# Crossbar transfers for the attention output of four batches, copies moved to ScalarE, and a new order, in a linear-attention and gated-convolution kernel

## The chip, the cores and the metric

The kernel runs on one core of one Trainium2 chip. A core has TensorE (PE, matrix products), VectorE (DVE), ScalarE (ACT), GpSimd (POOL) and SyncE (SP), which work side by side and wait for each other by semaphores; sixteen DMA engines move data for all of them. The metric is the device time of one execution in microseconds (us); lower is better. Several executions are timed, and one more view of one of them, a profile, lists every instruction with its start and duration.

## The reference

Two layers follow each other, over 8 batches of 576 positions. The first is attention by random features with 8 heads of 64 dimensions and 128 features; the second multiplies two projections with a third one that was convolved along the sequence.

```python
def phi(x):                       # q and k are scaled by D ** -0.25 before
    proj = einsum('bhsd,md->bhsm', x, omega)
    h = proj - sum(x * x, -1, keepdims=True) / 2
    return exp(h - max(h, -1, keepdims=True)) / sqrt(m)

q_p, k_p = phi(q_s), phi(k_s)
kv = einsum('bhsm,bhsd->bhmd', k_p, v)
z = sum(k_p, axis=2)
attn = einsum('bhsm,bhmd->bhsd', q_p, kv) / (einsum('bhsm,bhm->bhs', q_p, z)[..., None] + 1e-6)

x = attn.transpose(0, 2, 1, 3).reshape(B, S, H * D)
x1, x2, x3 = split(x @ w_proj, 3, axis=-1)
x2_conv = irfft(rfft(x2, axis=1) * rfft(filter_fft, axis=0)[None], n=S, axis=1)
out = (x1 * x2_conv * x3) @ w_out
```

All inputs and the output are float32; the kernel computes in bfloat16 with float32 sums.

## The kernel before

**The order of the work.** The kernel is written as two plain functions, `attention()` (line 931) and `hyena()` (line 1199). Neither sends an instruction to the chip. A recording layer, `Plan`, takes every call, with the stage and batch that the last `nc.at(stage, b)` named. `Plan.order` then gives each instruction a due time from its dependencies and from hand-set numbers by stage (`LEAD`), by stage and batch (`SHIFT`) and by stage and engine (`LEAN`), with `PERIOD`, `STRETCH` and `STAY` for the whole. `Plan.simulate` steps through a model of the engines and picks what goes next on each; `issue()` at line 383 sends the calls in that order. Each engine executes its own list in order, so an instruction that waits holds up all behind it on its engine. Because all calls are sent from one line, the profile has nearly all instructions at L388; they are told apart by the names of their tiles.

**Attention.** Of each batch 512 positions are the main part, four tiles of 128; the last 64 positions of two batches go together as one "left" tile. POOL loads `kn`, `qn`, `vn` (and `kl`, `ql`, `vl`) and casts them to bfloat16 on the way. Keys and queries must have their head dimension on the partitions, in `kt` and `qt`, for the feature products with `om2`. In batches 0 to 3 TensorE transposes them (`turn_keys`, `turn_queries`, through a PSUM bank named `t` and a copy). In batches 4 to 7 (`crossed`, line 310) a crossbar transfer, a DMA that transposes, does it from SP: `cross`, lines 951, 1020 and 1025. ScalarE takes the exponentials (`ek`, `eqt`). `max_to_c` finds the largest feature of each key, in the work tile `h1` with one buffer, and `scale_values` divides the values by it (`vc`). Key sums `kv` of 8 heads by 64 dimensions and one normaliser each, 520 columns, are copied out of PSUM at line 1119. `vcl`, `ekl` and `eql` are the same for the left tiles.

**Turning the output** (stage "turn out", lines 1146 to 1175). For each of the four tiles of a batch, eight matmuls make numerators and normaliser of eight heads in two PSUM banks (`two_banks`, tiles named `a`), and `normalise` (line 892) divides: a reciprocal and one multiplication on VectorE, into a tile `xb` of 128 positions by 512 channels. The second layer needs channels on the partitions, in `xt`. For batches 0 and 1 `turn_runs` does it by matmuls with a rearranged target; for batches 2 to 7 `turn_back` (line 908) makes eight transposes into one bank `t` for two tiles, and ScalarE copies 1,024 columns into `xt`.

**The second layer** goes by pairs of batches. `fold` and `fold_rest` add and subtract thirds of the sequence (`xf`, `xfl`), `project2` multiplies with the middle third of `wproj`, `forward` transforms by matmuls with tables, `spectrum` multiplies by the filter, the stage "inverse" transforms back, `gates` (line 1239) makes the product of the first and third projection (`x13`) from `xt` directly, and the stage "out" multiplies with `wout` and stores from `osb` tiles (three buffers), by SP. The filter is transformed once at the start (`filter_transform`); `split_out` (line 799) copies three of its results out of PSUM, a 128-row part on ScalarE and the negated lower half on VectorE, before SP moves them into `hps` and `hqs`.

**PSUM.** Matmul results stand in three single banks `h`, two pairs `a` and one bank `t`. A bank is free for the next product when ScalarE or VectorE has read it.

Of the kernel before, what the change touches and what calls it, by code (L numbers as in the profile page):

```python
# [11 lines left out]
FP32 = mybir.dt.float32  # L12
BF16 = mybir.dt.bfloat16
# [3 lines left out]
ALU = mybir.AluOpType  # L17
# [2 lines left out]

P = 128

PERIOD, STRETCH, STAY = 110.779, 7.132, 996.75
LEAD = {
    "cross keys": -8.69, "cross queries": -12.1, "filter": 3.6, "fold": 1.32, "forward": 26.46,
    "gates": -2.05, "inverse": 2.98, "keys": -44.78, "left keys": -2.87, "left out": -0.28,
    "left queries": 0.38, "load filter": -15.08, "load k": 17.16, "load kl": -0.85,
    "load q": 9.83, "load ql": -0.81, "load v": 8.12, "load vl": 0.04, "load w0": -1.42,
    "load w1": -2.9, "load w2": 1.71, "out": -19.09, "queries": -0.66, "residues": -3.04,
    "rest": -35.96, "start": -94.12, "sums": 14.75, "tables": -1.88, "turn out": 0.42,  # L30
    "turn queries": 4.98, "values": 204.41, "zeros": 3.6,
}

SHIFT = {
    ("forward", 0): -17.5, ("forward", 2): -35.59, ("forward", 7): 31.65, ("gates", 1): -47.99,
    ("gates", 2): -78.23, ("keys", 6): 46.62, ("keys", 7): 50.83, ("left queries", 1): -15.18,
    ("load kl", 0): -29.99, ("load ql", 0): 28.1, ("load v", 0): -89.26, ("queries", 6): -56.89,
    ("rest", 1): 278.3, ("rest", 7): 50.04, ("sums", 2): -15.61, ("sums", 6): -36.73,
    ("sums", 7): -24.35, ("turn out", 2): -115.3, ("turn out", 6): 1.26, ("values", 0): -174.25,
    ("values", 2): -204.34,  # L40
}
LEAN = {
    ("fold", "DVE"): -17.73, ("forward", "DVE"): 11.02, ("forward", "PE"): 2.87,
    ("gates", "PE"): 97.94, ("inverse", "DVE"): 14.74, ("keys", "PE"): -60.85,
    ("queries", "PE"): -5.83, ("rest", "PE"): -2.62, ("sums", "PE"): -3.28,
    ("turn out", "DVE"): -5.95, ("turn out", "PE"): -24.15,
}

SIZE = {FP32: 4, INT32: 4, BF16: 2, FP16: 2, mybir.dt.uint32: 4}
# [342 lines left out]
def kernel(  # L392
# [11 lines left out]
    nc = Plan(tc.nc, tc)  # L404
    B, H, S, D = q.shape
# [4 lines left out]
    NS = 2  # L410
    NT = 4
# [4 lines left out]
    CB = DM // P  # L416
# [3 lines left out]
    GAIN = 64.0  # L420
# [4 lines left out]
    att = ctx.enter_context(tc.tile_pool(name="att", bufs=1))  # L425
# [3 lines left out]
    def two_banks():  # L429
        return nc.tile(psum, [P, 2, 512], FP32, name="a2", bufs=2)  # L430
# [90 lines left out]
    for j in range(2):  # L521
        nc.vector.tensor_scalar_mul(
            out=om2[j * D : (j + 1) * D, :], in0=omt[:D, :MF], scalar1=qk_scale
# [32 lines left out]
    lo64, hi64 = slice(0, 64), slice(64, 128)  # L556

    residues = {}
# [240 lines left out]
    def split_out(ps, c):  # L799


        sc_ = nc.tile(hy, [P, 2, DM], BF16, name="osb", bufs=3)
        nc.scalar.mul(out=sc_[:, 0], in_=ps[:], mul=fsc[:, 0:1] if c == 1 else 2.0 * GAIN / S)
        nc.vector.tensor_scalar(
            out=sc_[hi64, 1], in0=ps[hi64, :], scalar1=-2.0 * GAIN / S, scalar2=None, op0=ALU.mult
        )
        moves = (
            (hps, slice(0, 64), 0, slice(0, 64)),
            (hps, slice(64, 128), 0, slice(0, 64)),
            (hqs, slice(0, 64), 1, slice(64, 128)),  # L810
            (hqs, slice(64, 128), 0, slice(64, 128)),
        )
        if c == 1:
            moves = (
                (hps, slice(0, 64), 0, slice(0, 64)),
                (hps, slice(64, 65), 0, slice(64, 65)),
                (hps, slice(65, 128), 0, slice(1, 64)),
                (hqs, slice(1, 64), 1, slice(65, 128)),
                (hqs, slice(65, 128), 0, slice(65, 128)),
            )  # L820
        for dst, rows, x, of in moves:
            nc.sync.dma_start(out=dst[rows, c, :], in_=sc_[of, x, :])
# [66 lines left out]
                out=ek_out, in_=ps[:].rearrange("p j (g m) -> p j g m", m=MF), func=AF.Exp  # L889
            )  # L890

    def normalise(ps):

        psh = ps[:, :, 0 : 4 * (D + 1)].rearrange("p a (h c) -> p a h c", c=D + 1)
        rden = nc.tile(att, [P, 2, 4, 1], FP32, name="rden", bufs=3)
        nc.vector.reciprocal(out=rden[:], in_=psh[:, :, :, D : D + 1])
        xb = nc.tile(att, [P, CB, P], BF16, name="xb", bufs=4)
        nc.vector.tensor_tensor(
            out=xb[:].rearrange("p c (g d) -> p (c g) d", d=D).rearrange(
                "p (a h) d -> p a h d", a=2  # L900
            ),
            in0=psh[:, :, :, 0:D],
            in1=rden[:].to_broadcast([P, 2, 4, D]),
            op=ALU.mult,
        )
        return xb
# [10 lines left out]
    def turn_runs(xt, xbs, c):  # L917


        ps = bank_t()  # L920
        for t in range(NT):
            nc.tensor.matmul(
                out=ps[:].rearrange("p (x t) -> p t x", t=NT)[:, t],
                lhsT=xbs[t][:, c],
                rhs=ident[:],
                start=True,
                stop=True,
            )
        nc.scalar.copy(out=xt[:, c, 0:SM], in_=ps[:])

    def attention():
        ekl = None
        for i in range(B // 2):
# [5 lines left out]
            for bb in range(2):  # L939
                b = 2 * i + bb  # L940
# [8 lines left out]
                crossed = b >= B // 2  # L949

                def cross(dst, src):
                    nc.sync.dma_start_transpose(out=dst, in_=src)
# [121 lines left out]
                for two in ((0, 1), (2, 3)):  # L1074
                    made = []
                    for pr in two:
                        ps = two_banks()
                        made.append((pr, ps))
                        for j in range(2):
                            nc.tensor.matmul(  # L1080
                                out=ps[:, j, :],
# [6 lines left out]
                                start=True,  # L1088
                                stop=True,
                            )  # L1090
                    for pr, ps in made:
                        nc.scalar.activation(
                            out=eqt[:, pr].rearrange("p j t c -> p j (t c)")
                            if b >= NS
                            else eqt[:, pr].rearrange("p h (u j) c -> p j (h u) c", j=2),
                            in_=ps[:]
# [6 lines left out]
                ps = two_banks()  # L1103
                for h in range(H):
                    half = ps[:, h // 4]
                    o = half[:, (h % 4) * (D + 1) : (h % 4 + 1) * (D + 1)]
                    nc.tensor.matmul(
                        out=o, lhsT=ekl[:, h, :], rhs=vcl[:, bb, h, 0 : D + 1], start=True, stop=False
                    )
                    for t in range(NT):  # L1110
                        nc.tensor.matmul(
                            out=o,
                            lhsT=ek[:, h, t, :],
                            rhs=vc[:, h, t, 0 : D + 1],
                            start=False,
                            stop=(t == NT - 1),
                        )
                kv = nc.tile(att, [P, 2, 4, D + 1], BF16, name="kv", bufs=3)
                nc.vector.tensor_copy(
                    out=kv[:],  # L1120
                    in_=ps[:, :, 0 : 4 * (D + 1)].rearrange("p a (h c) -> p a h c", c=D + 1),
                )
# [2 lines left out]
                if bb == 1:  # L1125
# [3 lines left out]
                    ps = two_banks()  # L1129
                    for j in range(2):  # L1130
                        nc.tensor.matmul(
                            out=ps[:, j, :],
                            lhsT=om2[rows[j]],
                            rhs=qlt[rows[j]].rearrange("p g s -> p (g s)"),
                            start=True,
# [3 lines left out]
                    for j in range(2):  # L1139
                        hs = slice(j * SL, (j + 1) * SL)  # L1140
                        nc.scalar.activation(
                            out=eql[:, j, :, hs].rearrange("p (g a) s -> p a g s", a=2),
                            in_=psf[:, :, :, hs],
# [3 lines left out]
                xt = nc.tile(hy, [P, CB, SM], BF16, name="xt", bufs=4)  # L1147
                xt_tiles[b] = xt
                xbs = []
                for t in range(NT):  # L1150
                    ps = two_banks()
                    for h in range(H):
                        nc.tensor.matmul(
                            out=ps[:, h // 4, (h % 4) * (D + 1) : (h % 4 + 1) * (D + 1)],
                            lhsT=eqt[:, h // 2, h % 2, t, :],
                            rhs=kv[:, h // 4, h % 4, :],
                            start=True,
                            stop=True,
                        )
                    xb = normalise(ps)  # L1160
                    xbs.append(xb)
                    if b < NS:
                        if t == NT - 1:
                            for c in range(CB):
                                turn_runs(xt, xbs, c)
                    elif t % 2 == 1:
                        turn_back(
                            xt[:, :, (t - 1) * P : (t + 1) * P].rearrange(
                                "p c (g x) -> p g c x", g=2
                            ),  # L1170
                            xbs,
                            "p (g c) x -> p g c x",
                            g=2,
                        )
                        xbs = []
# [4 lines left out]
            xtl = nc.tile(hy, [P, 2, CB, SL], BF16, name="xtl", bufs=2)  # L1180
            ps = two_banks()
            for h in range(H):
                o = ps[:, h // 4, (h % 4) * (D + 1) : (h % 4 + 1) * (D + 1)]
                for j in range(2):
                    nc.tensor.matmul(
                        out=o,
                        lhsT=eql[:, j, h, :],
                        rhs=kv_tiles[2 * i + j][:, h // 4, h % 4, :],
                        start=(j == 0),
                        stop=(j == 1),  # L1190
                    )
            xb = normalise(ps)
# [347 lines left out]
```

## Time and profile before

| | |
|---|---|
| median of six executions | 269.28 us (267.62 to 270.65) |
| the profiled execution | 267.79 us, of which the span from its first to its last instruction is 265.8 us |
| granted TensorE clock in it | 0.992 |
| matmuls, weight loads | 2,266 each |
| transposes of `xb` on TensorE | 144 |
| copies of `xt` out of bank `t` on ScalarE | 12 of 1,024 columns, 8 of 512 |
| crossbar transfers | 8, on SP |
| moved by POOL's queue | 17.31 MB |
| moved by SP's and ScalarE's queue | 16.94 MB |

The profile is of one execution; the time beside its span is what lies around the first and last instruction. A line of a group reads: line, engine, operation, target and sources, tile shape and count, then busy time in us and the mean duration in ns, then idle time of the engine just before these instructions and what ended it. A slice is a fortieth of the span, and its digit the busy tenths. The end of a matmul is modelled, and matmuls overlap, so the busy time of TensorE is not the sum of its durations.

### The profile page before, as it was taken

What the parts mean: (1) busy time and instruction counts of PE and PEld (TensorE: products, weight loads), DVE (VectorE), ACT (ScalarE), POOL (GpSimd) and SP (SyncE); (2) the same over time, 40 slices, a digit from 0 to 9 for tenths busy, and PEclk for the clock granted to TensorE, in tenths of its full rate; (3) what the DMA queues carried; (4) which work ended last, traced back from release to release, by engine and by line L of the source; (5) the groups of instructions that cost most, each with busy time, mean ns of one, the idle gap of its engine ahead of it and who ended that gap; (6) DMA issues with size and microseconds to landing.
All of it is one profiled execution on the core that took longest, in us unless ns stands there. A gap on an engine that the chain in (4) does not pass through costs nothing.

```text
span 265.8 us, 5830 instructions
## 1 busy us (share of the span) xinstructions
PE 242.7 (91%) x2266; PEld 137.4 (52%) x2266; DVE 221.8 (83%) x492; ACT 194.8 (73%) x301; POOL 62.7 (24%) x86
## 2 busy tenths in 40 slices
PE   0267679999999999999999999999999999999994
PEld 0255536665556566454566455444855555455541
DVE  7889998769977889999989776999999886378780
ACT  1797487676999968799755896999646966756633
POOL 8823662372557303151014000000000000000000
PEclk9997999999999999999999999999999999999999
DMA  6999999999999997999979352515613123101406
GB/s 78 190 198 198 160 202 209 203 171 147 123 136 157 202 170 43 172 162 149 276 120 167 78 107 94 118 57 154 137 34 121 39 95 102 44 22 38 159 1 197
DMA packets 84707, 34.74 MB, mean 131 GB/s; under 512 B 56139, under 2 KB 79176, under 8 KB 84680
## 3 DMA queue, kind: packets, MB, share of 16 engines
q0 software_dynamic: 59616, 17.31, 64.1%
q1 hardware_dynamic: 24920, 16.94, 27.6%
q8 instruction: 17, 0.28, 0.4%
q10 hardware_dynamic: 144, 0.13, 0.1%
q14 instruction: 10, 0.08, 0.1%
HBM read 34.64 MB, written 9.44 MB: 166 GB/s over the span
## 4 chain that ended last, share of the span: by engine, by line
PE 76%; DVE 15%; ACT 6%; issue 2%; ACTq 0%; DVEq 0%
PE h L388 58%; PE a L388 12%; PE t L388 5%; DVE h L388 2%; ACT eqt L388 1%; DVE yt L388 1%; DVE vcl L388 1%; DVE bt L388 1%; ACT L388 1%; DVE xb L388 1%; ACT yt L388 1%; DVE xf L388 1%; DVE vc L388 1%; DVE x L388 1%; DVE qt L388 1%
## 5 line engine op out<-in xcount | busy, mean ns | idle before, releaser
L388 PE MATMUL h<-xt,wproj 128*128 128x512 bf16 x256 | 62.0, 380 | 0.0
L388 ACT CAST x<-h 128x512 bf16<-128x512 f32 x68 | 40.2, 599 | 27.0 <-PE h L388 25.4
L388 PEld LDWEIGHTS <-wproj 128*128 128x128 bf16 x384 | 31.2, 99 | 26.2 <-issue 1.3
L388 ACT ACTIVATE ek<-a 128x1024 bf16<-128x1024 f32 x32 | 32.0, 1042 | 3.6 <-PE a L388 3.6
L388 ACT ACTIVATE eqt<-a 128x1024 bf16<-128x1024 f32 x32 | 32.1, 1048 | 1.8 <-PE a L388 1.8
L388 PE MATMUL h<-wproj,xf 128*128 128x512 bf16 x128 | 31.2, 379 | 0.0
L388 PE MATMUL h<-wout,yt 128*128 128x512 bf16 x128 | 30.1, 379 | 0.3 <-DVE yt L388 0.3
L388 ACT ACTIVATE osb<-h 128x512 f32<-128x512 f32 (+3 forms) x46 | 25.9, 573 | 4.5 <-PE h L388 2.9
L388 POOL DMA_DIRECT2D qn<-in_q_dram x26 | 22.9, 895 | 26.0 <-DMA qt<-qn 14.0
L388 DVE TENSOR_TENSOR x<-h,x 128x512 bf16<-128x512 f32 x32 | 22.0, 688 | 6.9 <-PE h L388 6.5
L388 DVE TENSOR_TENSOR xb<-a,rden 128x512 bf16<-128x512 f32 x36 | 23.3, 675 | 0.3
L388 DVE TENSOR_TENSOR bt<-h,osb 128x384 f16<-128x384 f32 x32 | 16.6, 553 | 3.7 <-PE h L388 2.0
L388 PEld LDWEIGHTS <-yt 128*128 128x128 bf16 x128 | 12.0, 98 | 14.7 <-DVE yt L388 0.8
L388 PEld LDWEIGHTS <-xf 128*128 128x128 bf16 x134 | 12.4, 99 | 12.4 <-PE a L388 0.4
L388 PE MATMUL h<-x,fwb 128*128 128x512 bf16 x72 | 18.3, 379 | 0.0
L388 PE MATMUL h<-gtab,xs 128*128 128x384 bf16 x64 | 15.6, 326 | 0.3 <-DVE bt L388 0.3
L388 ACT COPY xt<-t 128x1024 bf16<-128x1024 bf16 x12 | 12.2, 1019 | 4.4 <-PE t L388 4.2
L388 PE MATMUL t<-ident,xb 128*128 128x128 bf16 x144 | 13.7, 238 | 0.8 <-ACT xt L388 0.8
L388 PEld LDWEIGHTS <-eqt 128*128 128x128 bf16 x256 | 10.8, 98 | 5.5 <-DVE xb L388 1.2
L388 PE MATMUL a<-om,kt 64*128 64x128 bf16 x256 | 11.8, 226 | 1.4 <-DVE kt L388 1.0
L388 PE MATMUL a<-kv,eqt 128*128 128x65 bf16 x256 | 11.9, 194 | 1.3 <-DVE xb L388 0.9
L388 DVE RECIPROCAL rden<-a 128x8 f32<-128x8 f32 x36 | 7.0, 201 | 7.2 <-PE a L388 6.6
(167 smaller groups left out, 472.1 us busy)
## 6 DMA issues: line engine op xcount, KB each, us to landing
out_dram<-osb SPq DMA_DIRECT2D x24, 256.0 KB, 2.1
vn<-in_v_dram POOLq DMA_DIRECT2D x8, 512.0 KB, 9.8
kn<-in_k_dram POOLq DMA_DIRECT2D x7, 512.0 KB, 7.3
qn<-in_q_dram POOLq DMA_DIRECT2D x24, 128.0 KB, 8.7
sw<-sp SPq DMA_DIRECT2D x16, 128.0 KB, 3.8
wproj<-in_moe_w_proj_dram POOLq DMA_DIRECT2D x3, 512.0 KB, 8.2
qn<-in_q_dram POOLq DMA_DIRECT2D x2, 512.0 KB, 12.6
out_dram<-xf SPq DMA_DIRECT2D x4, 256.0 KB, 2.0
```

Source lines behind the costliest of these rows:

```text
L388: getattr(real, name)(*args, **kw)
```

## The change

The output of batches 4 to 7 is no longer turned by TensorE. `normalise` writes each of the four tiles of a batch into its part of one larger tile, which takes the name and the single buffer of `h1`; after the fourth, one crossbar transfer on SP writes all of `xt`. In PSUM the eight heads stand 128 columns apart, where they stood 65 apart, in all batches and in the left tiles. The copy of the key sums, and the negated filter copy of `split_out`, go from VectorE to ScalarE. All numbers of the planner are new, and with them the order on every engine, POOL's loads and SP's transfers included.

```diff
-PERIOD, STRETCH, STAY = 110.779, 7.132, 996.75
+PERIOD, STRETCH, STAY = 132.577, 8.076, 3059.83
 LEAD = {
...
+    "cross keys": -1.86, "cross out": 1.89, "cross queries": -0.95, "filter": -1.41,
...
 SHIFT = {
...
 LEAN = {
...
         sc_ = nc.tile(hy, [P, 2, DM], BF16, name="osb", bufs=3)
         nc.scalar.mul(out=sc_[:, 0], in_=ps[:], mul=fsc[:, 0:1] if c == 1 else 2.0 * GAIN / S)
-        nc.vector.tensor_scalar(
-            out=sc_[hi64, 1], in0=ps[hi64, :], scalar1=-2.0 * GAIN / S, scalar2=None, op0=ALU.mult
-        )
+        nc.scalar.mul(out=sc_[hi64, 1], in_=ps[hi64, :], mul=-2.0 * GAIN / S)
...
-    def normalise(ps):
+    def normalise(ps, xb=None):
 
-        psh = ps[:, :, 0 : 4 * (D + 1)].rearrange("p a (h c) -> p a h c", c=D + 1)
-        rden = nc.tile(att, [P, 2, 4, 1], FP32, name="rden", bufs=3)
-        nc.vector.reciprocal(out=rden[:], in_=psh[:, :, :, D : D + 1])
-        xb = nc.tile(att, [P, CB, P], BF16, name="xb", bufs=4)
+        psh = ps[:].rearrange("p a (h c) -> p (a h) c", c=P)
+        rden = nc.tile(att, [P, H, 1], FP32, name="rden", bufs=3)
+        nc.vector.reciprocal(out=rden[:], in_=psh[:, :, D : D + 1])
+        if xb is None:
+            xb = nc.tile(att, [P, CB, P], BF16, name="xb", bufs=4)[:]
         nc.vector.tensor_tensor(
-            out=xb[:].rearrange("p c (g d) -> p (c g) d", d=D).rearrange(
-                "p (a h) d -> p a h d", a=2
-            ),
-            in0=psh[:, :, :, 0:D],
-            in1=rden[:].to_broadcast([P, 2, 4, D]),
+            out=xb.rearrange("p c (g d) -> p c g d", d=D),
+            in0=psh[:, :, 0:D].rearrange("p (c g) d -> p c g d", g=2),
+            in1=rden[:].rearrange("p (c g) d -> p c g d", g=2).to_broadcast([P, CB, 2, D]),
             op=ALU.mult,
         )
         return xb
...
-                nc.vector.tensor_copy(
+                nc.scalar.copy(
                     out=kv[:],
                     in_=ps[:, :, 0 : 4 * (D + 1)].rearrange("p a (h c) -> p a h c", c=D + 1),
                 )
...
+                if crossed:
+                    xb4 = nc.tile(att, [P, CB, NT, P], BF16, name="h1", bufs=1)
                 for t in range(NT):
                     ps = two_banks()
                     for h in range(H):
                         nc.tensor.matmul(
-                            out=ps[:, h // 4, (h % 4) * (D + 1) : (h % 4 + 1) * (D + 1)],
+                            out=ps[:, h // 4, (h % 4) * P : (h % 4) * P + D + 1],
...
-                    xb = normalise(ps)
+                    xb = normalise(ps, xb4[:, :, t] if crossed else None)
                     xbs.append(xb)
-                    if b < NS:
+                    if crossed:
+                        if t == NT - 1:
+                            nc.at("cross out", b)
+                            cross(
+                                xt[:].rearrange("p c (t x) -> p (c t) x", t=NT),
+                                xb4[:].rearrange("p c t x -> p (c t x)"),
+                            )
+                    elif b < NS:
```

More of the change, by code (lines that the diff above doesn't have):

```diff
@@ L21 @@
 P = 128
-PERIOD, STRETCH, STAY = 110.779, 7.132, 996.75
+PERIOD, STRETCH, STAY = 132.577, 8.076, 3059.83
 LEAD = {
[L25 to L31, printed above, removed]
+    "cross keys": -1.86, "cross out": 1.89, "cross queries": -0.95, "filter": -1.41,
+    "fold": -1.38, "forward": 68.57, "gates": 0.52, "inverse": -1.95, "keys": 5.37,
+    "left keys": -0.11, "left out": -0.33, "left queries": 37.06, "load filter": -63.41,
+    "load k": -0.23, "load kl": -0.83, "load q": 0.19, "load ql": 1.42, "load v": 0.21,
+    "load vl": -0.15, "load w0": -1.83, "load w1": 5.49, "load w2": 1.25, "out": -1.99,
+    "queries": -0.43, "residues": 1.48, "rest": 0.66, "sines": 4.41, "start": -115.12,
+    "sums": 37.58, "tables": -1.3, "turn out": -0.79, "turn queries": -0.04, "values": 96.58,
+    "zeros": -0.01,
@@ L32 @@
 }
 SHIFT = {
[L35 to L40, printed above, removed]
+    ("fold", 0): -6.59, ("fold", 1): 51.34, ("forward", 1): -64.26, ("forward", 6): -65.11,
@@ new lines @@
+    ("forward", 7): -64.2, ("left keys", 2): 46.16, ("left queries", 7): -36.93,
+    ("load kl", 0): -35.9, ("load q", 0): 1.17, ("load v", 0): -95.34, ("load v", 1): 95.91,
+    ("load vl", 0): -20.54, ("out", 1): 148.99, ("queries", 1): 32.44, ("queries", 6): -10.06,
+    ("rest", 1): 255.75, ("rest", 7): 5.08, ("sums", 2): -41.35, ("sums", 6): -35.91,
+    ("sums", 7): -35.42, ("turn out", 1): 6.64, ("turn out", 2): -370.9,
+    ("turn queries", 0): -3.89, ("turn queries", 2): 31.07, ("values", 0): -72.86,
@@ L41 @@
+    ("values", 1): 308.0, ("values", 2): -98.35,
 }
 LEAN = {
[L43 to L46, printed above, removed]
+    ("fold", "DVE"): 3.25, ("forward", "PE"): 23.82, ("gates", "PE"): 78.43,
+    ("keys", "PE"): -26.62, ("rest", "DVE"): 4.62, ("rest", "PE"): -3.97, ("start", "POOL"): 0.17,
@@ L47 @@
+    ("turn out", "DVE"): 4.04, ("turn queries", "DVE"): 13.21,
 }
@@ L1182, in attention @@
             for h in range(H):
-                o = ps[:, h // 4, (h % 4) * (D + 1) : (h % 4 + 1) * (D + 1)]
+                o = ps[:, h // 4, (h % 4) * P : (h % 4) * P + D + 1]
                 for j in range(2):
```

## The prediction

> **What bounds the kernel now.** I read the page's busy totals and slices first, then busy time by stretch of the run, the chain of waits, the groups by form, and the crossbar transfers one by one.
>
> ```profile
> PE 242.7 (91%) x2266; PEld 137.4 (52%) x2266; DVE 221.8 (83%) x492; ACT 194.8 (73%) x301; POOL 62.7 (24%) x86
> ...
> PE   0267679999999999999999999999999999999994
> ...
> DVE  7889998769977889999989776999999886378780
> ACT  1797487676999968799755896999646966756633
> ```
>
> PE (TensorE) is the busiest engine, and from the eighth slice (46 us) on it is never idle for a tenth of a slice. Before that VectorE is fullest. The stretches say the same:
>
> ```profile
> 0.00:42.00 42.00, 23.23 (x277) 15.37 (x278) 37.68 (x105) 28.71 (x38) 25.02 (x40) 0.96 1.27 173
> 42.00:92.00 50.00, 50.00 (x519) 28.82 (x517) 40.16 (x80) 40.86 (x62) 24.01 (x31) 1.00 1.72 167
> 92.00:142.00 50.00, 49.64 (x535) 29.38 (x534) 46.88 (x100) 38.57 (x64) 12.93 (x17) 1.00 1.21 159
> 142.00:192.00 50.00, 49.99 (x452) 26.96 (x451) 43.32 (x91) 43.12 (x67) 0.70 (x1) 1.00 0.55 109
> ```
>
> Columns: length, then busy us of PE, weight loads, DVE, ACT and POOL. PE fills 50 of 50 us in each stretch after 42; before that DVE has 37.7 of 42. "Busy" hides short gaps, so I price PE by the spacing of matmul starts. The chain of waits shows it:
>
> ```profile
> 64.15 0.45 PE t L388 x8
> 64.60 1.73 PE h L388 x8
> ```
>
> Eight transposes take 0.45 us (56 ns each), eight matmuls with 512 columns 1.73 us (216 each). The starts in the trace give likewise 162 ns for 384 columns, 83 for 192, 31 for 65 columns, two 64-row matmuls side by side for the price of one, and 96 ns more at each change between 64 and 128 rows. The 2,266 matmuls and 84 such changes then come to 232.3 us. The last matmul starts at 261.7 us, where this sum stands at 232.0: 29.7 us were lost, **25.9 of them before 44 us and only 3.8 in the 218 us after**. So a matmul that goes is worth its full spacing, and there is little slack that a better order could still find late in the run.
>
> **What the Trainium skill says.** "TensorE: Matmul & The Clock Gate", section "Back-to-back issue gap", gives N/2.4 + 2.5 ns for one matmul: 56 ns at 128 columns, as measured here, and warns of 81 ns in a stream with weight loads, which this trace does not show. "DMA: Bandwidth & Descriptors", section "Issuing engines are not separate DMA queues": transfers of all engines run on the same 16 DMA engines and interleave. The trace agrees strongly:
>
> ```profile
> L388 SPq DMA_TRANSPOSE kt<-kn x1: 1606/1606/1606, 66.9 to 66.9; - x1
> DMA to landing us min/median/max: 14.3/14.3/14.3
> L388 SPq DMA_TRANSPOSE qt<-qn x1: 1352/1352/1352, 90.9 to 90.9; - x1
> DMA to landing us min/median/max: 11.9/11.9/11.9
> L388 SPq DMA_TRANSPOSE kt<-kn x1: 1802/1802/1802, 165.3 to 165.3; - x1
> DMA to landing us min/median/max: 4.3/4.3/4.3
> ```
>
> The same transfer lands 14.3 and 11.9 us after issue while POOL's loads run, 4.3 us once they are over. For a copy from PSUM on ScalarE, "VectorE: DVE Perf Modes", in its section on the TRN2 errata, has (172 + N)/1.2 ns: 577 for 520 columns, an estimate; the row of 512-column copies has 599, and I use 0.60.
>
> **The change part by part.**
>
> ```profile
> L388 PE MATMUL t<-ident,xb 128*128 128x128 bf16 x144 | 13.7, 238 | 0.8 <-ACT xt L388 0.8
> L388 ACT COPY xt<-t 128x1024 bf16<-128x1024 bf16 x12 | 12.2, 1019 | 4.4 <-PE t L388 4.2
> L388 DVE CAST kv<-a 128x520 bf16<-128x520 f32 x8 | 5.5, 696 | 0.3 <-PE a L388 0.2
> L388 DVE TENSOR_SCALAR osb<-h 64x512 bf16<-64x512 f32 x3 | 2.0, 692 | 0.1
> ```
>
> *Output turn of batches 4 to 7.* Each loses 16 of the 144 transposes and two of the 12 copies. PE: 64 x 0.056 = 3.6 us, all on the path. Bounds: 0, if a wait takes their place, and 64 x 0.095 = 6.1 us by the busy column. ScalarE: 8 x 1.02 = -8.2 us. Added: four crossbar transfers on SP, 4.3 to 14.3 us each.
>
> *Copies.* DVE loses 8 x 0.70 + 3 x 0.69 = 7.6 us; ScalarE gains 8 x 0.60 + 3 x 0.60 = 6.6, so it ends 1.6 us lighter.
>
> *Head spacing in PSUM (65 to 128 columns) and the target in `h1`.* Same instruction and element counts; the strided forms are not in the trace. Bounds: -0.1 to +0.2 us for each of 36 normalisations, on a DVE that gets 7.6 us lighter; taken as nothing, covered by the PE stream. With that cover gone it would cost up to 7 us of DVE time.
>
> *New order on PE.* The row changes go from 84 to 86: +0.2 us. **PE's work: 232.3 to 228.9, -3.4 us.**
>
> *New order, start.* PE is held until batch 1's key sums, which wait for the product of values and weights, done on DVE at 42.75 us after 27 us without a gap of note. Ahead of it the new order has one `kv` copy and three filter copies less: 0.70 + 2.0 = 2.7 us, so 40.1. But ScalarE gets that work: from batch 0's last query features (about 31.7 us, since `kv` now stands between them) to batch 0's last `xt` copy it has 16 pieces of about 0.54 and three of 0.95, 11.5 us, thus 43.2. There the PE sum stands at 19.0, a loss of 24.2 against 25.9. The filter's matmuls come ahead of these; for this POOL issues the filter loads before the weights. The last weight load then stands behind 6.4 MB, and at the 160 to 209 GB/s of these slices it has landed by about 35 to 38 us, wanted at 43. Gain 1.6 at best, -0.5 if ScalarE idles on the way; I take 0.9.
>
> *New order, the middle.* Between the first gates of batch 0 and the first key features of batch 4 ScalarE has 38.1 us of pieces beside 41.5 us of PE work (92%); before 36.3 beside 42.1. It ran 9.97 of 10 us in the stretch 84 to 94 without PE losing any. Taken as nothing; bound 3 us.
>
> *New order, crossbar transfers.* `kt` and `qt` have one buffer each, so a transfer starts after the last matmul on the old content. PE work between that and the first matmul on the new content was 22.1 us for the queries of batch 4 and is 12.1; for the keys of batch 5 it was 11.4 and is 5.4. Measured: 11.9 us for the first; for the second (issued at 108.2) the last packet ended after 6.3. That leaves waits of 0.2 and 0.9 to 1.3 us; if POOL's loads are past by then, none. Output of batch 4: 15.4 us of PE work and 13.0 of DVE work stand between the last sum and the first fold, loads of batch 7 run beside it, 0 to 1.5 us. Batch 5: DVE has only 1.7 us before the fold, so it idles some 3 us; PE has 13.2, none lost. Batches 6 and 7: quiet queue, 14.4 and 12.0 us, none; `h1`, which the key maxima share, is rewritten after 9.4 us of DVE work against 4.5. On SP the stores and batch 6's queries stand behind batch 4's transfer, which holds the queue 1.3 to 4.7 us; the three `osb` buffers cover that. I take 0.8 for all, bounds 0 and 4.
>
> Sum: -3.4 - 0.9 + 0.8 = -3.5 on the profiled execution (267.8 us, span 265.8 and 2.0 around it), so 264.3. The median of the six runs, 269.3, stands 1.5 above it: **265.8 us**. A measurement here can tell about 0.5% (1.35 us) from no change.
>
> **The rivals.**
> *A, the order gives the gain back in small waits* (20%): ScalarE at 92% up to PE-sum 61 costs its 3 us, or the start stays at 25.9. For it: DVE's tail pieces moved there, and 3.8 us of late loss is so little that a new order can hardly match it. Against: the stretch 84 to 94. -3.4 + 3 = -0.4: 268.9, within 0.5%.
> *B, the keys of batch 5 arrive late* (13%), which is slower. Place: `kt` turned over 103 us in, with 5.4 us of PE work behind it, in one queue with the queries of batch 4 and beside POOL's loads for batch 6. Should it land after 14.3 us like the first one, PE waits 14.3 + 0.3 - 5.4 = 9.2 us: -4.3 + 9.2 = +4.9, 274.2. It decides from about 9.4 us on. For it: two of the early landings were over 11. Against: POOL's queue thins out after 94 us (2.3 and 2.6 us busy in the two stretches to 116), and 6.3 measured.
> *C, the transposes were hidden* (5%): then only the start counts: -0.9, 268.4. Against: the chain lists them end to end with matmuls.
> The forecast has 62%, from 263.5 to 267.5.
>
> **Numbers.** Range 263.5 to 269.9: the forecast with its bounds, A and C; most of B is left out. Faster: the forecast, with small shares of A and C, 0.68; within 0.5%: the rest of these, 0.17; slower: B and a little of A, 0.15.
>
> **What would show it.** Matmuls 2,202, transposes of `xb` 80, no `xt` copy from `t` after batch 3; DVE near 214 us busy, ScalarE near 193. The first gates start near 43 us. The loss at the last matmul (start less 228.6 of work) is about 28 to 30 us. PE stays full at 100 to 112 and 150 to 166 us. A gap of PE behind `kt` or `qt` of over 3 us would mean B; ScalarE above 9.8 of 10 with PE waiting for `h` banks would mean A; a start after 45 us would break the second term.

## The result, and the profile after

The changed kernel takes 267.71 us (median of 29 executions, 264.38 to 272.37), the kernel before 269.40 in the same rounds, 1.7 us more. The ratio of the two is 0.991, with a 95% interval of 0.9887 to 0.9933: about 2.4 us faster. It leaves out the slow executions, those over 1.5% above the fastest of the same kernel, and the first of the two profiled executions below is one of these. Repeated later beside other kernels the changed kernel took 267.96 us, ratio 0.9926 (0.9897 to 0.9954).

The forecast was 265.8 us, 3.5 less than before. The sign is right and the range on record (263.5 to 269.9) holds, but the median lies 0.2 us above the narrower band that the prediction gave its own forecast (263.5 to 267.5). It is 1.9 us above the forecast by the medians, 1.1 by the ratio.

Two executions of the changed kernel were profiled: 268.96 us with a span of 267.1, and in the repeat 266.81 us with a span of 264.9. I read both, because they differ at the place that matters; the account rests on what both show.

From the page of the first: busy totals, then busy tenths and the granted clock in 40 slices.

```profile
PE 243.0 (91%) x2202; PEld 135.8 (51%) x2202; DVE 214.7 (80%) x481; ACT 194.4 (73%) x304; POOL 62.6 (23%) x86
...
PE   0376989999999998996999999999999999999994
...
ACT  1897798568998998984755957996668637746433
...
PEclk9998699999999999999799999999999999999999
```

VectorE (214.7) and ScalarE (194.4) are where the prediction put them (214 and 193), and 64 matmuls are gone. But TensorE's busy time did not fall (242.7 before), and its row has what the row of before does not have once the matmuls fill it: a 6, in the 19th slice (120 to 127 us). In the next slice the clock is 0.7. The groups of the two kernels by form follow, the first line being of the kernel before.

```profile
L388 DVE TENSOR_TENSOR xb<-a,rden 128x512 bf16<-128x512 f32 x36 | 23.3, 675 | 0.3
...
L390 PE MATMUL t<-ident,xb 128*128 128x128 bf16 x80 | 8.8, 253 | 0.7 <-ACT xt L390 0.6
...
L390 ACT CAST kv<-a 128x520 bf16<-128x520 f32 x8 | 4.7, 593 | 5.9 <-PE a L390 5.7
...
L390 DVE TENSOR_TENSOR h<-a,rden 128x512 bf16<-128x512 f32 x16 | 10.5, 675 | 0.1
...
L390 DVE RECIPROCAL rden<-a 128x8 f32<-128x8 f32 x36 | 7.0, 201 | 7.1 <-PE a L390 6.5
```

The operations themselves cost what was assumed: 80 transposes are left; a copy of key sums takes 593 ns on ScalarE (taken: 600); a normalisation with heads 128 columns apart takes 675 and 201 ns, as with 65 columns. So the missing time is in waits. As for the prediction, I set each matmul's start against the sum of spacings ahead of it. The loss up to that point, in us:

| profiled execution | at 50 us | at 120 | at 130 | last matmul |
|---|---|---|---|---|
| before | 25.9 | 27.6 | 28.0 | 29.7 |
| after, first | 25.0 | 28.0 | 31.8 | 34.1 |
| after, repeat | 24.6 | 27.2 | 29.2 | 32.0 |

TensorE's work is 228.6 us by this count against 232.0. The start gained 0.9 and 1.3 us. Then 3.8 and 2.0 us are lost between 120 and 130 us, where the kernel before lost 0.4. The timeline of the first execution (start, duration, engine, operation, in brackets the idle time before it and what ended it), SP, ScalarE and TensorE:

```profile
116.47 3.01 SPq L390 DMA_TRANSPOSE kt<-kn  x1
119.58 1.71 SPq L390 DMA_DIRECT2D out_dram<-osb  x2
...
122.98 0.59 ACT L390 CAST xs<-h 128x512 bf16<-128x512 f32 x1
125.99 0.48 ACT L390 CAST osb<-h 128x384 f16<-128x384 f32 x1 [2.42 <-DMA out_dram<-osb]
...
126.92 1.44 PE L390 MATMUL h<-x,fwb 128*128 128x512 bf16 x3 [2.11 <-ACT osb L390]
```

Read backwards: TensorE waits for an `h` bank that ScalarE has not emptied; ScalarE waits for one of the three `osb` buffers; that buffer still belongs to an output store; and SP issued this store only at 119.58 us, right after the transfer of the keys of batch 6 had held its queue for 3.01 us. ScalarE had written the stored rows at 116.20 to 116.80. The repeat shows the same pattern; the last line is of its list of waits (total, times, longest in us):

```profile
115.73 3.03 SPq L390 DMA_TRANSPOSE kt<-kn  x1
118.86 1.69 SPq L390 DMA_DIRECT2D out_dram<-osb  x2
...
124.98 0.48 ACT L390 CAST osb<-h 128x384 f16<-128x384 f32 x1 [2.15 <-DMA out_dram<-osb]
...
PE h L390 <- ACT osb L390: 2.5, 2, 1.8
```

The chain of waits of the first execution has the store and what follows it:

```profile
119.42 0.16 ACT x L390
119.58 6.32 DMA out_dram<-osb
...
125.99 0.88 ACT osb L390 x2
...
126.92 5.14 PE h L390 x20
```

Ahead of the store the chain names a copy on ScalarE, not the transfer. That is an inference of the view: in experiment 1 the same store goes out as soon as its rows are written. The store took 6.32 us from issue to landing (6.03 in the repeat), against a median of 2.3 for these stores. From 120.3 to 125.8 us the packets of a POOL load of `v` ran beside it. And the 20 matmuls after the gap took 5.14 us: for about 3 us they ran at half clock, which adds 1.6 to the 2.28 us that the gap cost (2.11 idle). In the repeat the gap cost 2.01 us (1.84 idle), and the clock stayed.

A place behind a transfer is not enough by itself, as the kernel before shows:

```profile
108.17 4.69 SPq L388 DMA_TRANSPOSE kt<-kn  x1
112.95 3.63 SPq L388 DMA_DIRECT2D out_dram<-osb  x2
```

In that order a store whose rows were ready at 108.4 us went out at 112.95 and landed 2.6 us later, and ScalarE waited for no buffer. So there are two suspects, the store's place behind the transfer and the loads beside it, and the rivals stay: many small waits, ScalarE's load, transposes that were hidden.

### The profile page after: what moved, and what is told of

It reads as the page before. It is cut to its first block, busy times and chain, and to the rows that moved or that the text cites. A ratio compares the mean times of both kernels' runs of the same rounds, so it can differ in the third digit from the quotient of the medians.

```text
span 267.1 us, 5693 instructions
## 1 busy us (share of the span) xinstructions
PE 243.0 (91%) x2202; PEld 135.8 (51%) x2202; DVE 214.7 (80%) x481; ACT 194.4 (73%) x304; POOL 62.6 (23%) x86
## 4 chain that ended last, share of the span: by engine, by line
PE 76%; ACT 8%; DVE 7%; DMA 5%; issue 2%; SPq 0%; ACTq 0%; DVEq 0%
PE h L390 58%; PE a L390 13%; PE t L390 5%; DMA out_dram<-osb 2%; DMA kt<-kn 2%; ACT eqt L390 2%; ACT osb L390 1%; DVE h L390 1%; ACT L390 1%; ACT yt L390 1%; DVE vcl L390 1%; DMA xw<-xr 1%; DVE kt L390 1%; ACT gtab L390 1%; DVE x L390 1%
## 5 line engine op out<-in xcount | busy, mean ns | idle before, releaser
L390 PEld LDWEIGHTS <-wproj 128*128 128x128 bf16 x384 | 31.0, 99 | 26.3 <-issue 2.3
L390 ACT ACTIVATE eqt<-a 128x1024 bf16<-128x1024 f32 x32 | 32.8, 1049 | 2.0 <-PE a L390 1.8
L390 ACT ACTIVATE osb<-h 128x512 f32<-128x512 f32 (+4 forms) x49 | 27.5, 566 | 8.4 <-PE h L390 5.9
L390 PE MATMUL h<-wproj,xf 128*128 128x512 bf16 x128 | 32.3, 387 | 0.0
L390 PE MATMUL h<-wout,yt 128*128 128x512 bf16 x128 | 30.9, 379 | 0.3 <-DVE yt L390 0.3
L390 PE MATMUL h<-x,fwb 128*128 128x512 bf16 x72 | 19.1, 389 | 2.1 <-ACT osb L390 2.1
L390 DVE TENSOR_TENSOR xf<-xt 128x1024 bf16<-128x1024 bf16 (+1 forms) x16 | 8.7, 553 | 7.8 <-ACT xt L390 4.6
L390 PE MATMUL a<-qt,om 64*128 64x512 bf16 x64 | 12.1, 410 | 1.9 <-DVE qt L390 1.2
L390 DVE TENSOR_TENSOR xb<-a,rden 128x512 bf16<-128x512 f32 x20 | 13.2, 676 | 0.3
L390 ACT CAST osb<-h 128x384 f16<-128x384 f32 x16 | 7.7, 481 | 7.8 <-PE h L390 5.3
L390 POOL DMA_DIRECT2D vn<-in_v_dram x8 | 7.2, 903 | 24.4 <-DVE vc L390 19.0
```

The costliest lines, as they stand in the source:

```text
L390: getattr(real, name)(*args, **kw)
```

## Experiments

All are edits of the changed kernel unless said otherwise. Edits marked "in `issue`" rearrange the planned list just before it is sent out, so that every other instruction keeps its place on its engine.

**1. The transfer behind the stores.** In `issue`:

```diff
-        for op in self.order():
+        ops = self.order()
+        moved = next(o for o in ops if o.where == ("cross keys", 6))
+        after = [o for o in ops[ops.index(moved) :] if o.eng == "SP"][2]
+        ops.remove(moved)
+        ops.insert(ops.index(after) + 1, moved)
+        for op in ops:
```

> The changed kernel; on SP the transfer that turns the keys of batch 6 is issued two stores later (behind the second of the stores that stood behind it), all else in the same order. Theory 1, the store is late because it stands behind that transfer in SP's queue: it is issued at about 117 us instead of 119.6, has landed by about 120, ScalarE's copy of the inverse stage no longer waits 2.4 us, TensorE loses neither the 2.3 us gap at 124.4 nor the 2 us at half clock after it, and the time is 2 to 4 us below that of the changed kernel (264 to 266 us). Theory 2, the store is late because the load of v runs beside it on the DMA engines: it still takes over 5 us from issue, the gap shrinks by at most the 2.7 us of earlier issue, and the time falls by less than 1 us. Theory 3, the missing 2 us are spread over the run: no change within 0.5 us.

Measured: 265.08 us, ratio to before 0.9839 (0.9792 to 0.9886). Busy time in two stretches of ten us (length, then PE, weight loads, DVE, ACT, POOL, granted clock, DMA share, GB/s), here and in the repeat of the changed kernel:

```profile
120.00:130.00 10.00, 10.00 (x111) 6.25 (x110) 9.59 (x20) 7.18 (x14) 0.00 (x0) 1.00 1.15 204
145.00:155.00 10.00, 7.83 (x61) 3.90 (x59) 7.61 (x16) 5.86 (x10) 0.00 (x0) 1.00 0.59 114
```

```profile
120.00:130.00 10.00, 8.16 (x59) 4.42 (x58) 7.88 (x18) 6.70 (x13) 0.00 (x0) 1.00 1.07 183
145.00:155.00 10.00, 9.85 (x75) 4.92 (x74) 9.61 (x21) 7.57 (x12) 0.00 (x0) 1.00 0.64 141
```

TensorE is full at 120 to 130 us. The first of the two stores went out at 116.00 us, as soon as its rows were written, and landed 2.7 us later. In this execution TensorE loses 2.2 us at 145 to 155 instead, and there the same pattern repeats: a store stands behind the output transfer of batch 4, which held SP for 6.06 us. That execution was the longest of its seven (267.07).

**2. A second transfer behind its store.** As 1, and the output transfer of batch 4 behind the one store that followed it.

```diff
+        moved = next(o for o in ops if o.where == ("cross out", 4))
+        after = [o for o in ops[ops.index(moved) :] if o.eng == "SP"][1]
...
```

> The changed kernel with two transfers moved on SP: the keys of batch 6 behind the two stores after it, as in keys6_later, and the output turn of batch 4 behind the one store after it. Theory: in keys6_later the second store then stood behind the output's transfer, which held the queue 6.06 us; ScalarE's next output copy waited 2.5 us for its buffer and TensorE lost 2.5 us at 148 to 150. With both moved, that goes too: 0.8 to 2.5 us below keys6_later, 262.6 to 264.3 us. Rival: the output of batch 4, issued later by some 2 to 3 us, is late for its fold and the gain turns into that wait: within 0.5 us of keys6_later (265.1).

Measured: 264.97 us, ratio 0.9834 (0.9785 to 0.9883). In the profile both stretches are full:

```profile
120.00:130.00 10.00, 9.94 (x117) 6.35 (x116) 9.58 (x21) 7.35 (x14) 0.00 (x0) 1.00 1.12 200
145.00:155.00 10.00, 10.00 (x83) 5.21 (x82) 9.83 (x24) 7.22 (x13) 0.00 (x0) 1.00 0.43 96
```

The loss at the last matmul is 29.3 us, less than before the change; 0.8 us of what it gains on the repeat stand ahead of 50 us, where the edit changes nothing. But the median equals that of experiment 1, and the 0.8 us or more that I expected did not come. Either the second wait is not in most executions of experiment 1, or its removal costs as much elsewhere; the profiles do not tell which.

**3. The stores on another queue, the transfer where it was.** In `issue`, the two stores go to ScalarE's queue, each one operation after its copy:

```diff
...
+            ops.insert(ops.index(after) + 1, o)
+            o.calls = [(self.nc.scalar, n, a, k) for _, n, a, k in o.calls]
```

> The changed kernel; the transfer of the keys of batch 6 stays where it is on SP, but the two output stores behind it are issued by ScalarE's queue, each one operation after the copy that fills its buffer. Theory 1, the place in SP's queue is what costs: the first store goes out at about 117.5 us, lands by 121, ScalarE does not wait for its buffer and the gap of 2 to 2.3 us at 124 us is gone; minus 2 for the gap, plus up to 0.8 for two issues of 0.37 us on ScalarE: 265.5 to 266.5 us. Theory 2, the packets of the transfer and of the loads are what costs, wherever the store is queued: it still takes over 5 us, the gap stays above 1 us, 267.5 to 268.5.

Measured: 265.78 us, ratio 0.9889 (0.9833 to 0.9944). The store on ScalarE's queue, and ScalarE's timeline:

```profile
115.79 0.39 ACTq L398 DMA_DIRECT2D out_dram<-osb  x1
...
121.95 0.59 ACT L398 CAST xs<-h 128x512 bf16<-128x512 f32 x1
122.44 0.48 ACT L398 CAST osb<-h 128x384 f16<-128x384 f32 x1
```

The store goes out at 115.79, while the transfer (115.44, 3.23 us) holds SP. The inverse stage's copy follows its neighbour without a wait, and TensorE has 9.93 of 10 us busy. The transfer's packets ran beside the store, which landed after 4.1 us, still early enough. By time alone this kernel is not told apart from the changed one (the intervals overlap); by the trace it is.

**4. The loads beside the stores, first try.** In `issue`, POOL's load of `v` of batch 6 is put behind that of batch 7.

> The changed kernel with SP's order as it is; on POOL the load of v of batch 6, whose packets ran at 120.3 to 125.8 us beside the two late stores, is issued 16 us later, behind the load of v of batch 7 (wanted after 165 us). If the stores behind the transfer were late by their place alone: issued at 119 us as before, they land after 2.3 us more, at about 122, just in time for the copy at 123, so the gap at 124 falls to 0 to 0.5 us only if the load had its part; it stays at 2 us if the place alone counts. Time 265.5 to 266.5 in the first case, 267.7 in the second; the loads that now bunch at 134 to 146 us may slow the output's transfer of batch 4 and cost up to 1.5 us again.

Measured: 267.89 us, ratio 0.9947 (0.9918 to 0.9977), and ScalarE's wait is still there (2.48 us). But the edit missed its aim: POOL still issued one 512 KB load at 117.55 us, the other one of the two. The load beside the stores was not taken away, so this says nothing on whether the loads matter.

**5. The loads beside the stores, second try.** Both loads of `v` go behind POOL's loads of the queries of batch 7, which wait for a buffer until 128.6 us.

```diff
+        loads = [o for o in ops if o.where in (("load v", 6), ("load v", 7))]
+        last = [o for o in ops if o.where == ("load q", 7)][-1]
...
```

> The changed kernel with SP's order as it is; on POOL the loads of v of batches 6 and 7 are put behind the four loads of the queries of batch 7. Those wait until the transfer of batch 5's queries has read its buffer (about 130 us), so no load runs at 120 to 126 us beside the two late stores (in v6_load_later the two loads of v only changed places). If the stores were late because of the loads as well as of their place: issued at 119.6 us behind the transfer, they land within 3 us, at about 122.5, ahead of the copy at 123, the gap at 124 falls below 0.5 us, time 265 to 266.5. If the place in the queue alone is enough: the copy still waits over 1 us, the gap stays over 1 us, 267 to 268.5. A late v of batch 6 (wanted after 165 us, landed by about 150) should cost nothing; the bunched loads beside batch 4's output transfer may cost up to 1.5 us.

Measured: 270.35 us, ratio 1.0027 (1.0002 to 1.0053), 3.2 +- 0.9 us more than the changed kernel by the ratios. SP and ScalarE:

```profile
115.02 3.04 SPq L397 DMA_TRANSPOSE kt<-kn  x1
118.15 1.67 SPq L397 DMA_DIRECT2D out_dram<-osb  x2
...
135.39 7.39 SPq L397 DMA_TRANSPOSE xt<-h  x1
142.88 0.53 SPq L397 DMA_DIRECT2D out_dram<-osb  x1
...
121.52 0.59 ACT L397 CAST xs<-h 128x512 bf16<-128x512 f32 x1
122.00 0.48 ACT L397 CAST osb<-h 128x384 f16<-128x384 f32 x1
...
150.21 0.60 ACT L397 ACTIVATE osb<-h 128x512 f32<-128x512 f32 x1 [4.47 <-DMA out_dram<-osb]
```

At 122 us the wait is gone, though the store still stood 3 us behind the transfer: it landed 2.2 us after its issue. So **the wait at 124 us needs both**: three microseconds of queue (experiments 1 and 3 take them away) and a slow landing beside a load (this one does). The queue alone fits into the time that three buffers give. For the slow landing alone this is an estimate: issued at 116.0 us as in experiment 1, and landing after 6.3, the store would have been done at 122.3, ahead of the copy at 122.65. The loads, moved to 128.6 to 134 us, then met batch 4's output transfer, which held SP for 7.39 us, and the store behind it kept ScalarE waiting 4.47 us: the same pattern, dearer. The clock fell after that gap of 2.88 us idle.

**6. Both cures.** Experiments 2 and 4 in one kernel.

> The changed kernel with the two transfers behind the stores (as in stores_first) and the load of v of batch 6 later (as in v6_load_later). Expected 264 to 265.5 us: TensorE's late loss is already down to 4.5 us in stores_first, and the load can only help the crossbar transfers at 120 to 126 us or hinder that at 138 us. More than 0.5 us below stores_first would say that the loads still cost something there.

Measured: 265.20 us, ratio 0.987 (0.9823 to 0.9916), like experiment 2. As the load's part was void, it is a repeat of 2. (Counted from 50 us, as in the table, the late loss of experiment 2 was 5.4 us, not 4.5.) By time alone this repeat is not told apart from the changed kernel either.

**7. TensorE's work put back.** Four matmuls of `ident` with itself, which nobody reads, ahead of each of the 16 output groups:

```diff
                     ps = two_banks()
+                    if crossed:
...
+                        for c in range(CB):
+                            nc.tensor.matmul(
+                                out=ps[:, 0, c * P : (c + 1) * P], lhsT=ident[:], rhs=ident[:],
...
```

> The changed kernel with TensorE work that nobody reads added: four 128x128 matmuls ahead of each of the 16 output matmul groups of batches 4 to 7, 64 in all, as many as the change takes away; every engine's order stays. If TensorE's stream sets the end: 64 x 56 ns = 3.6 us slower than the changed kernel, 271.3 us. If the transposes were hidden beside other work (rival C): no change within 0.5 us, 267.7. Anything between tells what share of TensorE's work is on the path.

Measured: 271.96 us, ratio 1.0088 (1.0053 to 1.0123). Against the changed kernel that is 0.0178 of 269.4 us, 4.8 us, give or take 1.1 (the two half-widths, as independent). The last matmul starts 3.95 us later than in the repeat (264.56 against 260.61), for 3.58 us of added work: as near as two single executions tell, all of it is on the path. Rival C falls. The median says rather more than the work; what the rest is stays open.

**8. The copies of key sums back on VectorE**, in `issue`, at the same place of the list:

```diff
+            if o.where[0] == "sums" and o.eng == "ACT" and o.name.startswith("copy kv"):
+                o.calls = [(self.nc.vector, "tensor_copy", a, k) for _, _, a, k in o.calls]
```

> The changed kernel with the eight copies of key sums back on VectorE, at the same place in the order; ScalarE 4.8 us lighter, VectorE 5.5 us fuller. Forecast's view: only the copy ahead of the start counts, 0 to 0.7 us slower (267.7 to 268.4). Rival A, ScalarE's load in the middle of the run costs the missing 2 us: 1 to 3 us faster (265 to 267). If VectorE was the tighter of the two in the middle too: 2 us slower or more.

Measured: 268.75 us, ratio 0.9982 (0.9958 to 1.0006), 1.9 +- 0.9 us more than the changed kernel. Rival A's ScalarE half expected it faster. The loss by matmul starts is 0.5 us larger than in the repeat at 50 us, which is no more than executions differ (23.9 to 25.0 us in five profiles whose start is the same). It is 1.1 larger at 90, where TensorE has lost 0.5 waiting for a `kv` copy on VectorE, and 1.8 at 120, where a wait for the keys of batch 5 (0.69) comes in.

**9. The filter copies back on VectorE**, likewise.

> The changed kernel with the three filter copies back on VectorE at the same place in the order. Both VectorE and ScalarE end close to each other ahead of the start. If VectorE sets the start: 3 x 0.7 = 2.1 us more on it, of which the 0.9 us measured gain of the start goes, 0.9 to 1.5 us slower. If ScalarE sets it: 0 to 1 us faster. The part after 50 us keeps its gap at 124 us either way.

Measured: 269.89 us, ratio 1.0002 (0.9971 to 1.0032), 2.5 +- 1.0 us more. The loss at 50 us is 26.3, outside the 23.9 to 25.0 of those five profiles: back on VectorE, the copies delay the start.

**10. The old numbers of the planner with the new operations, and 11. the new numbers with the kernel before.**

```diff
-PERIOD, STRETCH, STAY = 132.577, 8.076, 3059.83
+PERIOD, STRETCH, STAY = 110.779, 7.132, 996.75
...
```

> The changed kernel's operations (crossbar turns, copies on ScalarE) with the planner's old numbers, so the old plan for the new work. TensorE's work is 228.9 us as with the new numbers. If the new numbers were needed: stalls of several us, 268 us or more, slower than the changed kernel. If they add little: 266 to 268 us.

> The kernel before, its transposes and its copies on VectorE, with the planner's new numbers: the new plan for the old work. TensorE's work is 233.6 us (98 changes of row mode against 84, so 1.3 us more than before). If the new numbers bring a gain of their own (start 0.9 us): about 269.5, equal to before. If they suit only the new work: 272 us or more.

Measured: 279.65 us (ratio 1.0359, 1.0301 to 1.0417) and 278.53 us (1.033, 1.0284 to 1.0376). Both are far slower than either whole kernel. Operations and order are one thing here: neither has a worth of its own that could be added up.

**12. The changed kernel again**, for the second profile used above.

> The changed kernel itself once more, for a second profiled execution beside these runs. Expected 267.7 us (266.5 to 268.5), and again a gap of TensorE of 0.9 to 2.3 us behind the inverse stage's copy at about 124 us; the half clock after it is expected only if the gap is over 2.2 us, since three executions of its variants with gaps of 0.9, 1.9 and 2.2 us kept the full clock.

Measured: 267.96 us; the gap cost 2.01 us, and the clock stayed.

## Why the prediction was right, and where it was 1.9 us off

**TensorE's work, -3.4: right.** The loss table has it, and experiment 7 shows that such work is paid in full.

**Start, -0.9: right in size, as far as single executions tell, and its cause too.** 0.9 and 1.3 us in the two profiles. That VectorE, relieved of the filter copies, lets it through is what experiment 9 undoes. The copies were worth more than the term says, once the order counted on them: put back, the three filter copies cost 2.5 us and the eight of key sums 1.9. I had costed `kv` on VectorE beyond the start at nothing.

**Normalisation, ScalarE in the middle, crossbar arrivals: right.** 675 and 201 ns are unchanged. ScalarE cost no 3 us. The queries of batch 4 landed 6.6 us after issue (5.0 in the repeat) and were not waited for; the keys of batch 5 landed after 5.25 and cost about 0.1 us (up to 0.7 in the executions of the experiments), so rival B did not come. Batch 5's fold kept VectorE waiting 3.2 us, as foreseen (2.9 in the repeat), at no cost to TensorE.

**Waits, +0.8: the step that failed.** The text saw the stores and said: "the three `osb` buffers cover that". It said so for the transfer of batch 4's output and did not ask it of the keys of batch 6, whose transfer also went ahead of two stores; and it counted the time that a transfer holds SP, but not that the store behind it then lands beside a load, in 6.32 us (6.03 in the repeat) in place of 2.3. The late loss (from 50 us to the last matmul) was 3.8 us before and 7.4 in the repeat: +3.6 where +0.8 was put down. Of it 2.0 is this gap, 0.8 one wait of the inverse stage for its `h` bank at 102 us, which no experiment touched, and the rest is many small ones. The sign that the prediction named for its waits, a loss of 28 to 30 us at the last matmul, was missed too: 32.0 and 34.1. In the first profile the half clock made it +5.3. With -3.4 and -1.3 the repeat adds up to -1.1, which is how much earlier its last matmul starts (260.6 against 261.7). This is a comparison of two executions, and the one profiled before was 1.5 us below its median; so the sum explains the forecast's error of these two, 266.81 us against 264.3, better than it explains the median.

So the expected gain came, and a wait that the change itself built gave back 2.0 of the 4.7 us in the repeat (3.8 of 4.3 in the first profile). The four kernels whose two stores no longer stand behind that transfer (1, 2, 3, 6) have medians of 265.0 to 265.8 us, where the forecast was; each alone is told apart from the changed kernel only in experiments 1 and 2, and there barely. By the medians the result lies nearer to rival A (268.9) than to the forecast, by the ratio (2.4 us of 3.5) nearer to the forecast. A's doubt that a new order could match the late loss of 3.8 us was right. Its mechanism, a full ScalarE, fits at most the 0.8 us at 102 us, just before which ScalarE worked without a pause (100.9 to 102.7 us in the repeat). In the gap at 124 us it waited and was not full (6.70 of 10 us at 120 to 130 in the repeat).

Experiment 2 has the lowest median, 264.97 us, 1.7% below the kernel before; the interval of its ratio ends where that of the changed kernel begins (0.9883 and 0.9887). What stays open: how often the gap comes and how often the clock falls after it, since each kernel was profiled once or twice; why the second wait of experiment 1 did not show in the medians; the wait at 102 us; and the last microsecond of experiment 7.

## What to carry to other kernels

A transfer that moves work off the busiest engine also occupies the queue that issues it. List what stands behind it there, and follow each item to the buffer that it frees and the engine that wants this buffer next; then ask the same with the landing time of a busy stretch, not the median. A place in the queue and a slow landing can add up to a wait where one of them alone would not; here issuing what frees a buffer ahead of what is wanted late removed it, with every other engine's order as it was.

## What the runs showed of the hardware

**A short gap can cost the clock.** Idle times of TensorE of 0.73 (experiment 9), 1.77 (7), 1.84 (the repeat) and 1.99 us (8) left its clock at full rate; idle times of 2.11 us (first profile), 2.17 (4) and 2.88 (5) were followed by half clock, in the first profile with 512-column matmuls 427 ns apart in place of 216. Two short ones close together went both ways: 1.06 and 0.54 us, after smaller ones, were followed by half clock in the kernel with the old numbers (10), and 0.91 and 1.24 us in experiment 1 were not. The Trainium skill, "TensorE: Matmul & The Clock Gate", section "What's actually happening" in Part 1, says that the clock falls after an idle window of about 3.4 us; here 2.11 us of idling was enough in one execution, and 1.99 was not in another.

**Another queue, the same DMA engines.** The Trainium skill, "DMA: Bandwidth & Descriptors", section "Issuing engines are not separate DMA queues", says that issuing from another engine saves only the time on the sequencer and that this is usually small beside the transfer itself. Here it was not small: the transfer ahead of the store held SP for 3.23 us in experiment 3, the store itself took 4.1, and the time saved was enough to remove the wait.

**How long a crossbar transfer holds its queue differs widely.** All moved 512 KB, and they held SP for 1.32 to 7.39 us. POOL's loads beside them are not the whole reason: in the kernel before, the transfer at 90.9 us held SP for 1.35 us beside such loads, though it landed only after 11.9; in the first profile the one at 160.7 us held it for 2.97 us with none. What sets the time stays open.
